# Up projections from seven products of halves instead of eight, the shared ones in the recurrent cell's PSUM banks, with program order kept to the end

## Chip, cores, metric

One core of a Trainium2 chip. The metric is the time of one execution in microseconds (us) on the device. A time "of n runs" is the median, with the lowest and highest behind it. All runs quoted were of the fast state except one run of `unpinned`, which is left out of its ratio. All times below are us unless another unit stands there; "step 20" is the pass of the main loop with s = 20 (counted from 0).

In the profile lines PE is TensorE (PEld its weight loads), DVE VectorE, ACT ScalarE, POOL GpSimd, SP the engine that issues most DMA; L92 is line 92 of the kernel. A record is one line of the trace: a 128x256 matmul leaves two. "Granted clock" is the share of full clock that TensorE was given.

## The reference

A gated recurrent cell (mLSTM) over 4 sequences of 768 tokens and 8 heads of 40 feeds a feed-forward block:

```python
def _moe_ref(x, w1, w2, w3, w_out):        # x: 3072 x 320, the output of the cell
    a = x @ w1                             # 320 x 1024
    b = x @ w2
    h = a * b @ w3                         # 1024 x 1024
    return (h @ w_out).astype(np.float32)  # 1024 x 320
```

The cell's part, cut to what matters: per token C = f C + i v k^T, then h = C q, a normaliser and an output gate. The kernel does it in chunks of 64 tokens with matmuls, and folds w3 @ w_out into one matrix of 1024 x 320 (`w3o`), so what is left of the feed-forward block is two "up" products, a product of the two, and one "down" product.

## The kernel before

TensorE's instructions are held in program order by the helper `mm`; the other engines' order is kept only up to the 17th step (`pinned`), after which a scheduler may move them. Two kinds of PSUM space matter: four banks in one tile `cell`, and four separate banks handed out in turn by `mps`.

```python
    cell = ps_c.tile([P, 4, 512], FP, name="cell", tag="cell")      # one tile, four banks
    ...
    def up(gr, fs, cs):                    # two blocks of 128 features, 256 tokens, both weights
        ...
        pa, pb = mps([128, len(fs), n], "pa"), mps([128, len(fs), n], "pb")
        for p, wt in ((pa, w1), (pb, w2)):
            for i, f in enumerate(fs):
                for cc in range(KF):       # 320 inputs = 128 + 128 + 64; the 64 come in up_rest
                    mm(p[:, i, :], wt[:, cc, f * 128:(f + 1) * 128], x[:, cc, cs], start=(i == cc == 0), stop=False)
        return pa, pb, x, gr, fs, cs

    def up_rest(pa, pb, x, gr, fs, cs):
        ...                                # the 64-row remainders, then
        nc.scalar.mul(out=a_sb, in_=pa, mul=UP ** -2)
        nc.vector.tensor_tensor(out=ab_t[gr][j][...], in0=pb, in1=a_sb, op=OP.mult)

    def ffn_out(gr, j):                    # a "down"
        po = mps([P, DM], "po")
        for f in range(FO):
            mm(po, ab_t[gr][j // 2][:, f, ...], w3o[:, f, :], start=(f == 0), stop=(f == FO - 1))
        o_sb = ffn.tile([P, DM], FP, name="o_sb", tag="o_sb", bufs=2)
        nc.scalar.copy(out=o_sb, in_=po)
        nc.scalar.dma_start(out=out[t0:t0 + P, :], in_=o_sb)
    ...
    n_up = [0] * 4 + [1] * 2 + [2] * 23 + [0]
    n_down = [0] * 17 + [2] * 10 + [0, 0, 4]
    pinned, ahead = 17, 9
    for s in range(len(n_up)):
        ...
        for _ in range(n_down[s]):
            ffn_out(*downs.pop(0))
        now = [ups.pop(0) for _ in range(n_up[s])]
        open_ups = [up(*x) for x in now]
        ...
        if s <= NU:
            gated = quarter_work(s, rest)  # the remainders, then the cell's matmuls and their readers
```

Of the kernel before, what the change touches and what calls it, by code (L numbers as in the profile page):

```python
# [8 lines left out]
FP = mybir.dt.float32  # L9
U32 = mybir.dt.uint32  # L10
AF = mybir.ActivationFunctionType
OP = mybir.AluOpType
UP = 2.0 ** 8
# [3 lines left out]
def kernel(  # L17
# [26 lines left out]
    nc = tc.nc  # L44

    B, H, S, D = q.shape
    L = 64
    P = 128
    NT = S // L
    NT2 = S // P  # L50
    NU = NT2 * B
# [3 lines left out]
    DM = H * D  # L55
    BH = B * H
    DFF = moe_w1.shape[1]
    FO = DFF // P
    KF = DM // P
    REM = DM - KF * P  # L60
    GT = B
    TG = GT * P
    NG = NU // GT
# [13 lines left out]
    def mps(shape, name):  # L77
        pool = banks.pop(0)
        banks.append(pool)
        return pool.tile(shape, FP, name=name, tag="m")  # L80
# [10 lines left out]
    def mm(out, lhsT, rhs, start=True, stop=True):  # L91
        in_order(nc.tensor.matmul(out, lhsT=lhsT, rhs=rhs, start=start, stop=stop))  # L92
# [4 lines left out]
    halves = [slice(0, L), slice(L, P)]  # L97
# [187 lines left out]
    def turn(n):  # L285


        if n >= N_DVE:
            for src, dst, name in zip(turned_in[n % 2], (kT_t, qT_t), ("kT", "qT")):
                dst[n] = sb.tile([128, NP, P], FP, name=name, tag=name)  # L290
                done = nc.vector.transpose(out=dst[n].rearrange("i p (r f) -> i p f r", f=4),
                                           in_=src[:, 32:TB].rearrange("i (p f d) -> i p f d", p=NP, f=4)[:, :, :, 0:32])
            return done
        for src, dst, name in ((kbuf[n % NB], kT_t, "kT"), (qbuf[n % NBQ], qT_t, "qT")):
            pt = mps([128, NP, P], "pt")
            for p in range(NP):
                transpose(pt[:, p, :], src[:, 2 * p:2 * p + 2, :].rearrange("p a b -> p (a b)"))
            dst[n] = sb.tile([128, NP, P], FP, name=name, tag=name)
            nc.scalar.copy(out=dst[n], in_=pt)
# [276 lines left out]
    def up_rest(pa, pb, x, gr, fs, cs):  # L576
        for i, f in enumerate(fs):
            for j, e in quarters:
                mm((pa, pb)[j][halves[e], i, :], wr[halves[j], f * 128 + e * L:f * 128 + (e + 1) * L],
                   x[halves[j], KF, cs], start=False, stop=(i == len(fs) - 1))  # L580
        j, t0 = divmod(cs.start, 2 * P)
        a_sb = ffn.tile([128, len(fs), cs.stop - cs.start], FP, name="a_sb", tag="a_sb")
        nc.scalar.mul(out=a_sb, in_=pa, mul=UP ** -2)  # L583
        nc.vector.tensor_tensor(out=ab_t[gr][j][:, fs[0]:fs[-1] + 1, t0:t0 + a_sb.shape[-1]], in0=pb, in1=a_sb, op=OP.mult)  # L584

    def ffn_out(gr, j):
        po = mps([P, DM], "po")
        for f in range(FO):
            mm(po, ab_t[gr][j // 2][:, f, j % 2 * P:(j % 2 + 1) * P], w3o[:, f, :], start=(f == 0), stop=(f == FO - 1))
        o_sb = ffn.tile([P, DM], FP, name="o_sb", tag="o_sb", bufs=2)  # L590
        nc.scalar.copy(out=o_sb, in_=po)  # L591
        t0 = j * S + gr * P
        nc.scalar.dma_start(out=out[t0:t0 + P, :], in_=o_sb)
# [1 line left out]

    ups = [(0, [f, f + 1], slice(j * 2 * P, (j + 1) * 2 * P)) for part in range(0, FO, FO // 2) for j in range(2)
           for f in range(part, part + FO // 2, 2)]
    ups += [(gr, [f, f + 1], slice(j * 2 * P, (j + 1) * 2 * P)) for gr in range(1, NG) for j in range(2)
            for f in range(0, FO, 2)]
    downs = [(gr, j) for gr in range(NG) for j in range(GT)]  # L600
    n_up = [0] * 4 + [1] * 2 + [2] * 23 + [0]
    n_down = [0] * 17 + [2] * 10 + [0, 0, 4]
    w12 = [("w12", i, part) for part in range(2) for i in range(2 * KF + 1)]
    todo = w12[KF * 2 + 1:] + [("wo", i, 0) for i in range(FO)] + [("w3", ko, part) for ko in range(FO) for part in range(2)]
    n_cvt = [2, 1, 1, 1, 2, 2, 3, 3, 3] + [2] * 7
    pinned, ahead = 17, 9
    behind = ExitStack()
    turned, converted, fetched = 0, 2, 2 * KF + 1

    for s in range(len(n_up)):  # L610
        if B <= s + 3 < NU:
            load_u(s + 3)
        if s + 2 < NU:
            load(s + 2)
            load_o(s + 2)
        if 0 < s < B - 1:
            weights(s + 1)
            out_gate(s)
        if s < NU:
            weighted(s)  # L620
            if s >= B:
                decayed(state[s % B][1], state[s % B][0], s, 0)
            if 0 < s < N_DVE:
                turn(s)
        if NY <= s - 2 < NU:
            send(s - 2)
        elif 0 <= s - 2 < NY:
            twice(s - 2)
        if NY <= s - 2 < NU:
            get_back(s - 2)  # L630
        while turned < min(s - 2, NY):
            x_trans(turned)
            turned += 1
        fold()
        for _ in range(n_down[s]):
            ffn_out(*downs.pop(0))
        now = [ups.pop(0) for _ in range(n_up[s])]
        open_ups = [up(*x) for x in now]
        if len(now) == 1 and turned == s - 2 < NY:
            x_trans(turned)  # L640
            turned += 1

        def rest():
            for x in open_ups:
                up_rest(*x)

        gated = None
        if s <= NU:
            gated = quarter_work(s, rest)
        else:  # L650
            rest()
        with tc.issue_after(gated.ins) if gated else nullcontext():
            if NY <= s - 2 < NU:
                x_turn(s - 2)
            if N_DVE <= s + 1 < NU:
                gated = turn(s + 1)
        if s == 0:
            gate_cols(g, gT, nc.scalar.copy)
            out_gate(0)
            scale_next()  # L660
            weights(1)
        if s == NU:
            cell_psum.close()
            banks.append(ctx.enter_context(tc.tile_pool(name="ps_x", bufs=4, space=bass.MemoryType.PSUM)))
        if B - 1 <= s < NU:
            if s + 1 < NU:
                weights(s + 1)
            out_gate(s)
        with tc.issue_after(gated.ins) if N_DVE <= s + 1 < NU else nullcontext():
            for _ in range(n_cvt[s] if s < len(n_cvt) else 0):  # L670
                convert()
                converted += 1
        if s >= ahead:
            while pend and len(scaled) < 2:
                scale_next()
        if N_DVE <= s + 2 < NU:
            load_turned(s + 2)
        while todo and fetched < converted + (2 if s < 2 else 3 if s < ahead - 1 else 4):
            fetch(*todo.pop(0))
            fetched += 1  # L680
        if s + 1 == pinned:
            for ins in keep_order(front):
                behind.enter_context(tc.issue_after(ins))
    behind.close()
    assert not ups and not downs and not todo and not pend and not turned_w3 and not ready_w3, (len(ups), len(downs), len(todo), len(pend))
# [1 line left out]
_INS = ['q', 'k', 'v', 'i_gate', 'f_gate', 'o_gate', 'moe_w1', 'moe_w2', 'moe_w3', 'moe_w_out']  # L687
_OUTS = [((3072, 320), 'float32')]
# [25 lines left out]
```

## Time and profile before

| | before |
|---|---|
| time, 3 runs (a fourth came with the result below) | 466.43 (465.67 to 467.24) |
| span of the profiled run | 464.6 |
| TensorE busy | 442.8 (95%) |
| VectorE busy | 262.6 (57%) |
| ScalarE busy | 134.4 (29%) |
| TensorE's share of the chain that ended last | 90% |

These lines are of the profile page of the kernel before: the slices (40 of 11.6 each, busy tenths), the granted TensorE clock in tenths, and the chain that ended last.

```profile
PE   2797989999999999999999999999999999999997
DVE  6758898899988988898823360624516134011110
PEclk9757999999999999999999999999999999999999
PE 90%; DVE 3%; SPq 2%; DMA 2%; issue 1%; POOL 1%; ACT 0%; ACTq 0%; DVEq 0%
```

From the seventh slice to the last but one TensorE has no gap that a tenth would show, and VectorE is lightly used in the second half. So TensorE's work is what the time consists of, and VectorE looks as if it had room. Both readings are right; neither says what happens when VectorE's results are asked for *between* two matmuls.

### The profile page before, as it was taken

Reading aid. Unit: us, or ns where it says so; the run is one execution under the profiler, and the core shown is the slowest. Engines: PE = TensorE matmul, PEld = TensorE weight load, DVE = VectorE, ACT = ScalarE, POOL = GpSimd, SP = SyncE. Lnnn points to the kernel's source line nnn. Section 1 sums busy time; section 2 is a strip of 40 time slices with the busy share of each in tenths; the row PEclk is TensorE's granted clock in tenths of the full one; section 3 lists DMA queues with packets and bytes.
Section 4 is the critical chain, followed back from the end, with each engine's and each line's share of the span. In section 5 each row is a group of like instructions: output and inputs, shape, how many; then the busy total and the mean of one; then the engine's idle time right before and its main releaser. Section 6 shows DMA issues by size and latency. Waiting matters only on the chain.

```text
span 464.6 us, 12788 instructions
## 1 busy us (share of the span) xinstructions
PE 442.8 (95%) x5319; PEld 356.1 (77%) x5319; DVE 262.6 (57%) x515; ACT 134.4 (29%) x376; POOL 82.6 (18%) x156
## 2 busy tenths in 40 slices
PE   2797989999999999999999999999999999999997
PEld 2686878888778887878778777787777877778864
DVE  6758898899988988898823360624516134011110
ACT  3743545444244134313641231211101101011110
POOL 5522333233220222022151120210000000000000
PEclk9757999999999999999999999999999999999999
DMA  8989978887988677676452635545021120200001
GB/s 174 182 163 173 204 156 159 158 194 174 204 185 195 151 141 171 171 153 141 89 134 58 142 65 123 111 92 118 17 64 32 32 64 1 62 16 14 1 14 44
DMA packets 136554, 52.72 MB, mean 113 GB/s; under 512 B 109936, under 2 KB 127536, under 8 KB 136496
## 3 DMA queue, kind: packets, MB, share of 16 engines
q1 hardware_dynamic: 132896, 47.87, 50.6%
q10 hardware_dynamic: 3600, 4.03, 2.5%
q8 instruction: 42, 0.69, 0.6%
q14 instruction: 16, 0.13, 0.1%
HBM read 46.07 MB, written 5.80 MB: 112 GB/s over the span
## 4 chain that ended last, share of the span: by engine, by line
PE 90%; DVE 3%; SPq 2%; DMA 2%; issue 1%; POOL 1%; ACT 0%; ACTq 0%; DVEq 0%
PE pa L92 27%; PE po L92 23%; PE pb L92 18%; PE cell L92 12%; PE wp L92 7%; DMA q_all<-in_q_dram 2%; PE pt L95 2%; SPq L128 1%; PE px L95 1%; SPq L173 1%; DVE h L380 0%; DVE pw L354 0%; POOL pw L282 0%; DVE h L376 0%; SPq L459 0%
## 5 line engine op out<-in xcount | busy, mean ns | idle before, releaser
L584 DVE TENSOR_TENSOR ab<-pb,a_sb 128x512 f32<-128x512 f32 x48 | 32.7, 689 | 137.7 <-ACT a_sb L583 137.6
L92 PE MATMUL po<-w3o,ab 128*128 128x320 f32 x384 | 106.2, 435 | 0.0
L92 PEld LDWEIGHTS po<-w3o,ab 128*128 128x128 f32 x384 | 72.1, 190 | 30.0 <-ACT a_sb L583 0.4
L92 PE MATMUL pa<-xT,w 128*128 128x256 f32 x384 | 91.0, 380 | 0.6 <-ACT xT L438 0.6
L92 PE MATMUL pb<-xT,w 128*128 128x256 f32 x384 | 90.7, 379 | 0.0
L92 PEld LDWEIGHTS pa<-xT,w 128*128 128x128 f32 x384 | 72.3, 190 | 13.0 <-ACT xT L438 0.9
L92 PEld LDWEIGHTS pb<-xT,w 128*128 128x128 f32 x384 | 73.0, 190 | 9.9
L583 ACT ACTIVATE a_sb<-pa 128x512 f32<-128x512 f32 x48 | 28.7, 598 | 172.0 <-PE pb L92 172.0
L309 POOL TENSOR_TENSOR state<-state,decay 128x164 f32<-128x164 f32 x40 | 19.3, 483 | 208.1 <-DVE den L388 157.8
L92 PE MATMUL pb<-xT,wr 64*64 64x256 f32 x384 | 47.0, 383 | 0.0
L92 PE MATMUL pa<-xT,wr 64*64 64x256 f32 x384 | 47.0, 383 | 0.0
L280 ACT ACTIVATE pw<-pw,aT 128x64 f32<-128x64 f32 x160 | 40.3, 336 | 15.8 <-DMA pw<-U_d 15.8
L92 PEld LDWEIGHTS pa<-xT,wr 64*64 64x64 f32 x384 | 25.8, 132 | 16.8 <-issue 7.8
L282 POOL TENSOR_SCALAR_AFFINE_SELECT pw<-pw 64x512 f32<-64x512 f32 x48 | 34.6, 722 | 14.3 <-ACT pw L280 12.7
L92 PE MATMUL wp<-wo,w3T 128*128 128x320 f32 x128 | 35.9, 433 | 1.1 <-DVE ab L584 1.1
L591 ACT COPY o_sb<-po 128x320 f32<-128x320 f32 x24 | 10.2, 423 | 78.8 <-PE po L92 74.9
L92 PEld LDWEIGHTS cell<-vbuf,pw 64*64 64x64 f32 x768 | 27.9, 143 | 6.1 <-DVE state L367 2.9
L92 PEld LDWEIGHTS wp<-wo,w3T 128*128 128x128 f32 x128 | 23.7, 190 | 10.2 <-DVE ab L584 1.4
L92 PE MATMUL cell<-vbuf,pw 64*64 64x41 f32 x768 | 27.9, 233 | 2.3 <-DVE state L367 2.3
L92 PEld LDWEIGHTS pb<-xT,wr 64*64 64x64 f32 x384 | 25.8, 132 | 0.0
L376 DVE TENSOR_TENSOR h<-cell,gT 128x328 f32<-128x328 f32 x24 | 12.0, 498 | 23.4 <-PE cell L92 23.4
L380 DVE TENSOR_TENSOR h<-cell,h 64x328 f32<-64x328 f32 x48 | 23.9, 497 | 1.1
(90 smaller groups left out, 465.7 us busy)
## 6 DMA issues: line engine op xcount, KB each, us to landing
raw<-in_moe_w_dram SPq DMA_DIRECT2D x64, 128.0 KB, 3.2
pw<-U_d SPq DMA_DIRECT2D x40, 128.0 KB, 3.9
kbuf<-in_k_dram SPq DMA_DIRECT2D x24, 160.0 KB, 4.5
vbuf<-in_v_dram SPq DMA_DIRECT2D x24, 160.0 KB, 4.8
o_in<-in_o_gate_dram SPq DMA_DIRECT2D x24, 160.0 KB, 4.5
out_dram<-o_sb ACTq DMA_DIRECT2D x24, 160.0 KB, 2.1
raw<-in_moe_w_dram SPq DMA_DIRECT2D x7, 512.0 KB, 5.8
raw<-in_moe_w_out_dram SPq DMA_DIRECT2D x32, 80.0 KB, 3.1
```

Source lines behind the costliest of these rows:

```text
L92: in_order(nc.tensor.matmul(out, lhsT=lhsT, rhs=rhs, start=start, stop=stop))
L95: in_order(nc.tensor.transpose(out, in_, ident[0:n, 0:n]))
L128: nc.sync.dma_start(out=dst, in_=rows(src, n))
L173: nc.sync.dma_start(out=dst, in_=src)
L280: nc.scalar.activation(out=pw[:, h, :], in_=src[:, h, :], func=AF.Exp, bias=aT[:, c, b * H + h:b * H + h + 1])
L282: nc.gpsimd.affine_select(out=pw[r], in_=pw[r], compare_op=OP.is_ge, fill=0.0, base=0, pattern=[[0, H], [1, L]], channel_multiplier=-1)
L309: nc.gpsimd.tensor_tensor(out=new, in0=old, op=OP.mult, in1=decay[:, b * NP:(b + 1) * NP, 2 * c + x:2 * c + x + 1] .to_broadcast([P, NP, D1]))
L376: nc.vector.tensor_tensor(out=h.rearrange("p (n two) d -> p two n d", two=2), in0=pi, in1=gT[:, c, hs].rearrange("p (n two) -> p two n", t ...
L380: nc.vector.tensor_tensor(out=h[r], in0=ph[x], in1=h[r], op=OP.add)
L583: nc.scalar.mul(out=a_sb, in_=pa, mul=UP ** -2)
L584: nc.vector.tensor_tensor(out=ab_t[gr][j][:, fs[0]:fs[-1] + 1, t0:t0 + a_sb.shape[-1]], in0=pb, in1=a_sb, op=OP.mult)
L591: nc.scalar.copy(out=o_sb, in_=po)
```

## The change

The intent: for the last three groups of 512 tokens, a 2 x 2 split of each up product (halves of the inputs, halves of the features against halves of the tokens) is done with seven products of halves instead of eight. Sums of weights and of tokens are formed ahead on VectorE. Three of the seven go straight into the result's banks ("single"); four are "shared" between several results: `p15` (a pair) and `p67` (a pair) per weight. They are read out, scaled and added by ScalarE and VectorE. The shared pairs need four more banks, and the change takes those of `cell`. What is read out is kept in the memory of the tile `wo`, and the sums lie in that of `raw` and `w3T`, so the profile shows these names. Program order is kept to the end (`pinned = 32`). The core of the diff, cut:

```diff
+        def shared():
+            p15, p67 = [bank(2 + j) for j in range(2)], [bank(j) for j in range(2)]
+            for j in range(2):
+                mm(p15[j][:, 0], of(j, 0, 0), B11, stop=False)
+                mm(p15[j][:, 1], sum_of(j, 0), T[0], start=False)
+                if j:
+                    nc.scalar.copy(out=kept[j][:, 0:4:3], in_=p15[j])                  # L646
+                else:
+                    nc.scalar.mul(out=kept[j][:, 0:4:3], in_=p15[j], mul=UP ** -2)     # L648
+            for j in range(2):
+                mm(p67[j][:, 0], sum_of(j, 1), T[1], stop=False)
+                mm(p67[j][:, 1], sum_of(j, 2), T[2], start=False)
+                for i in range(2):
+                    add(j, kept[j][:, 1 + i], p67[j][:, i], kept[j][:, i])             # L629, L631
+                nc.vector.tensor_tensor(out=kept[j][:, 1:4:2], ...)                    # L654
...
+        def product():
+            for t, a in zip(ab_t[gr], (lo, hi)):
+                nc.vector.tensor_tensor(out=t[...], in0=t[...], in1=a, op=OP.mult)     # L672
-    n_up = [0] * 4 + [1] * 2 + [2] * 23 + [0]
-    n_down = [0] * 17 + [2] * 10 + [0, 0, 4]
+    n_up = [0] * 4 + [1] * 2 + [2] * 11 + [0] * 15
+    n_seven = [0] * 19 + [1] * 12 + [0]
+    n_down = [0] * 17 + [2, 3, 2, 2, 2, 1] + [1] * 8 + [4]
-    pinned, ahead = 17, 9
+    pinned, ahead = 32, 9
...
+            if s <= NU:
+                seven[0]()          # single
+            seven[1]()              # shared
+        for i in range(n_down[s]):
+            ffn_out(*downs.pop(0), cell[:, 2 + i, 0:DM] if seven and s <= NU else None)
```

The line numbers in the comments were added here; the profile of the changed kernel names these lines. The last line matters: with the shared pairs in `cell`, the downs of these steps go into `cell` too.

More of the change, by code (lines that the diff above doesn't have):

```diff
@@ L584, in up_rest, with weight_sums @@
         nc.vector.tensor_tensor(out=ab_t[gr][j][:, fs[0]:fs[-1] + 1, t0:t0 + a_sb.shape[-1]], in0=pb, in1=a_sb, op=OP.mult)
-    def ffn_out(gr, j):
-        po = mps([P, DM], "po")
+    FH, TH = FO // 2, 2 * P
+    S_t, T_t = {}, {}
+    aside = wo.rearrange("p f d -> p (f d)")
+    def weight_sums(j):
+        mem = [wst.tile([128, CW, 2], U32, name="raw", tag="raw", bufs=4).rearrange("p n two -> p (n two)").bitcast(FP)
+               for _ in range(2)]
+        S1, S2, S3, S4 = S_t[j] = [m[:, i * CW:(i + 1) * CW] for m in mem for i in range(2)]
+        (A11, A21), (A12, A22) = ([(w1, w2)[j][:, cc, i * CW:(i + 1) * CW] for i in range(2)] for cc in range(KF))
+        for dst, p, q, op in ((S1, A21, A22, OP.add), (S2, S1, A11, OP.subtract), (S3, A11, A21, OP.subtract),
+                              (S4, A12, S2, OP.subtract)):
+            nc.vector.tensor_tensor(out=dst, in0=p, in1=q, op=op)
@@ new lines, in token_sums, with up_by_seven, of, sum_of @@
+    def token_sums(gr):
+        mem = wst.tile([128, FO, 128], FP, name="w3T", tag="w3T").rearrange("p k c -> p (k c)")
+        T1, T2, T3, T4 = T_t[gr] = [mem[:, i * TH:(i + 1) * TH] for i in range(4)]
+        (B11, B12), (B21, B22) = ([x_t[gr][:, cc, i * TH:(i + 1) * TH] for i in range(2)] for cc in range(KF))
+        for dst, p, q in ((T1, B12, B11), (T2, B22, T1), (T3, B22, B12), (T4, B21, T2)):
+            nc.vector.tensor_tensor(out=dst, in0=p, in1=q, op=OP.subtract)
+    def up_by_seven(gr, f, bank):
+        x, T = x_t[gr], T_t[gr]
+        (B11, B12), (B21, B22) = ([x[:, cc, i * TH:(i + 1) * TH] for i in range(2)] for cc in range(KF))
+        block, kept = {}, [aside[:, j * 4 * TH:(j + 1) * 4 * TH].rearrange("p (i t) -> p i t", i=4) for j in range(2)]
+        lo, hi = (ffn.tile([128, 2, TH], FP, name="a_sb", tag="a_sb") for _ in range(2))
+        def of(j, cc, i):
+            return (w1, w2)[j][:, cc, i * CW + f * 128:i * CW + (f + 1) * 128]
+        def sum_of(j, i):
+            return S_t[j][i][:, f * 128:(f + 1) * 128]
+        def add(j, out, p, q):
+            if j:
+                nc.vector.tensor_tensor(out=out, in0=p, in1=q, op=OP.add)
+            else:
+                nc.vector.scalar_tensor_tensor(out=out, in0=p, scalar=UP ** -2, in1=q, op0=OP.mult, op1=OP.add)
+        def single():
+            for j in range(2):
+                C1, C2 = block[j] = mps([128, 2, TH], "pa"), mps([128, 2, TH], "pb")
+                mm(C1[:, 0], of(j, 1, 0), B21, stop=False)
+                mm(C1[:, 1], of(j, 1, 1), T[3], start=False, stop=False)
+                mm(C2[:, 0], sum_of(j, 3), B22, stop=False)
+        def shared():
[3 more added lines that the diff above has]
+                mm(p15[j][:, 1], sum_of(j, 0), T[0], start=False)
+                if j:
+                    nc.scalar.copy(out=kept[j][:, 0:4:3], in_=p15[j])
+                else:
+                    nc.scalar.mul(out=kept[j][:, 0:4:3], in_=p15[j], mul=UP ** -2)
+            for j in range(2):
+                mm(p67[j][:, 0], sum_of(j, 1), T[1], stop=False)
+                mm(p67[j][:, 1], sum_of(j, 2), T[2], start=False)
+                for i in range(2):
+                    add(j, kept[j][:, 1 + i], p67[j][:, i], kept[j][:, i])
+                nc.vector.tensor_tensor(out=kept[j][:, 1:4:2], in0=kept[j][:, 1:3],
+                                        in1=kept[j][:, 3:4].to_broadcast([128, 2, TH]), op=OP.add)
+        def left():
+            if gr not in ab_t:
+                ab_t[gr] = [ffn.tile([128, FO, TH], FP, name="ab", tag="ab", bufs=6) for _ in range(2)]
+            for t in range(2):
+                for i in range(2):
+                    for j, e in quarters:
+                        c0 = (f + i * FH) * 128 + e * L
+                        mm(block[j][t][halves[e], i], wr[halves[j], c0:c0 + L], x[halves[j], KF, t * TH:(t + 1) * TH],
+                           start=False, stop=(i == 1))
+            for j, dst in enumerate(((lo, hi), [t[:, f:FO:FH, :] for t in ab_t[gr]])):
+                add(j, dst[0], block[j][0], kept[j][:, 0:3:2])
+                add(j, dst[1], block[j][1], kept[j][:, 1:4:2])
+        def product():
+            for t, a in zip(ab_t[gr], (lo, hi)):
+                nc.vector.tensor_tensor(out=t[:, f:FO:FH, :], in0=t[:, f:FO:FH, :], in1=a, op=OP.mult)
+        return single, shared, left, product
@@ L588, in ffn_out @@
+    def ffn_out(gr, j, po=None):
+        if po is None:
+            po = mps([P, DM], "po")
         for f in range(FO):
@@ L597 @@
            for f in range(part, part + FO // 2, 2)]
-    ups += [(gr, [f, f + 1], slice(j * 2 * P, (j + 1) * 2 * P)) for gr in range(1, NG) for j in range(2)
+    ups += [(gr, [f, f + 1], slice(j * 2 * P, (j + 1) * 2 * P)) for gr in range(1, 3) for j in range(2)
             for f in range(0, FO, 2)]
     downs = [(gr, j) for gr in range(NG) for j in range(GT)]
-    n_up = [0] * 4 + [1] * 2 + [2] * 23 + [0]
-    n_down = [0] * 17 + [2] * 10 + [0, 0, 4]
+    sevens = [(gr, f) for gr in range(3, NG) for f in range(FH)]
+    n_up = [0] * 4 + [1] * 2 + [2] * 11 + [0] * 15
+    n_seven = [0] * 19 + [1] * 12 + [0]
+    n_down = [0] * 17 + [2, 3, 2, 2, 2, 1] + [1] * 8 + [4]
     w12 = [("w12", i, part) for part in range(2) for i in range(2 * KF + 1)]
@@ L634 @@
         fold()
-        for _ in range(n_down[s]):
-            ffn_out(*downs.pop(0))
+        seven = None
+        if n_seven[s]:
+            seven = up_by_seven(*sevens.pop(0), (lambda i: cell[:, i].rearrange("p (i t) -> p i t", i=2)) if s <= NU else
+                                lambda i: mps([128, 2, TH], "p67" if i < 2 else "p15"))
+            if s <= NU:
[3 more added lines that the diff above has]
+            ffn_out(*downs.pop(0), cell[:, 2 + i, 0:DM] if seven and s <= NU else None)
+        if seven and s > NU:
+            seven[0]()
         now = [ups.pop(0) for _ in range(n_up[s])]
@@ L645, in rest @@
                 up_rest(*x)
+            if seven:
+                seven[2]()
         gated = None
@@ L652 @@
         with tc.issue_after(gated.ins) if gated else nullcontext():
+            if seven:
+                seven[3]()
             if NY <= s - 2 < NU:
@@ L656 @@
                 gated = turn(s + 1)
+            if s in (16, 17):
+                weight_sums(s - 16)
+            if s - 2 in range(4 * GT - 1, NU, GT):
+                token_sums((s - 2) // GT)
         if s == 0:
@@ L684 @@
     behind.close()
-    assert not ups and not downs and not todo and not pend and not turned_w3 and not ready_w3, (len(ups), len(downs), len(todo), len(pend))
+    assert not ups and not sevens and not downs and not todo and not pend and not turned_w3 and not ready_w3, (len(ups), len(downs), len(todo), len(pend))
 _INS = ['q', 'k', 'v', 'i_gate', 'f_gate', 'o_gate', 'moe_w1', 'moe_w2', 'moe_w3', 'moe_w_out']
```

## The prediction

> **What bounds the kernel now.** I read the page's engine summary first, then the chain that ended last in order of time, then the timeline of one step and of the tail. All times are us. TensorE is busy 95% of the span and carries 90% of the chain. From 230 on the chain is one unbroken row of TensorE work:
>
> ```profile
> 290.00 2.30 PE cell L92 x117
> 292.30 8.81 PE po L92 x32
> 301.11 1.73 PE pa L92 x8
> 302.83 1.73 PE pb L92 x8
> 304.56 1.73 PE pa L92 x8
> 306.29 1.73 PE pb L92 x8
> 309.90 2.29 PE cell L92 x104
> ```
>
> Columns: start, length, engine, tile, records. A step of this stage is 19.9: the recurrent cell 2.3, two down projections 8.81, two up blocks 6.9 and the 64-row remainders of the up blocks (309.90 less 308.02 = 1.88). Nothing waits, so each TensorE us saved there is a us of the end, and each new TensorE wait is one too. An up matmul of 128x256 is two records, eight records take 1.73: 0.432 per matmul. A down projection is 16 records, about 4.36 with its share of the gaps.
>
> The second thing to see is how the tile "cell" is waited for. It is one tile of four PSUM banks. Early in the run, where TensorE isn't backed up, the timeline shows:
>
> ```profile
> 37.67 1.01 DVE L380 TENSOR_TENSOR h<-cell,h 64x328 f32<-64x328 f32 x2
> ...
> 40.36 0.28 DVE L367 TENSOR_TENSOR state<-cell,state 128x164 f32<-128x164 f32 x1
> ...
> 40.69 1.83 PE L92 MATMUL cell<-vbuf,pw 64*64 64x41 f32 x30 [2.29 <-DVE state L367]
> ```
>
> The matmuls starting at 40.69 write banks 2 and 3, whose readers (L376, L380) had ended at 38.68. Yet they waited for L367, which reads bank 1. So the program orders accesses to cell as one tile, not bank by bank. In before this costs nothing later, because 17.6 of po, pa and pb stand between two uses of cell.
>
> Handoff costs, from the tail of the timeline:
>
> ```profile
> 443.98 17.49 PE L92 MATMUL po<-w3o,ab 128*128 128x320 f32 x64
> 444.10 0.60 ACT L583 ACTIVATE a_sb<-pa 128x512 f32<-128x512 f32 x1 [0.27 <-PE pb L92]
> ...
> 448.59 0.43 ACT L591 COPY o_sb<-po 128x320 f32<-128x320 f32 x1 [3.89 <-PE po L92]
> ```
>
> The first po takes to about 448.39 (443.98 + 0.1 + 4.31), its copy starts 448.59: 0.20 from TensorE to ScalarE. DVE to TensorE is 0.05 (40.64 to 40.69), and the first weight load after a wait costs about 0.1 more (a group at 425.99 took 1.83 for the usual 1.73). A 128x512 PSUM eviction on ScalarE is 0.60.
>
> [...] in 38 to 40 TensorE was busy 0.40 of 2.00 and in 42 to 44 the granted clock was 0.50, while an idle 1.5 around 61 left it at 1.00.
>
> **The change part by part.** *Removed:* each of the 12 new blocks (512 tokens, two weights) uses 14 products of 128x256 where two old steps' worth of the same work used 16; the remainders are equal. 24 x 0.432 = **10.4 off** TensorE. ScalarE loses 24 a_sb evictions.
>
> *Added on VectorE:* per block six shared adds (four of 256 columns, two of 512: 4 x 0.42 + 2 x 0.69 = 3.1), four adds of 512 (2.8), two products (1.4), less two old products (1.4): +5.9. With cell work 4.6 and turns 2.8 a step is about 14.6 on VectorE, beside 19.0 on TensorE with two downs (14 x 0.432 + 8.81 + 1.88 + 2.30), 14.6 with one. No throughput bound except near step 22, but order matters. Weight and token sums lie in steps 16, 17, 21, 25, beside TensorE work.
>
> *Moved:* there are now 32 steps. Six blocks (steps 19 to 24) put four pairs of shared products and the downs in cell's banks. I read the semaphore values in the built program: there each group waits for the reader of the group before, although in another bank. In order on TensorE:
> - first p15 waits for the last state add of the previous cell. In the step of 272 the cell's matmuls ended at 272.32, L359 at 274.98 and L367 at 275.98: 3.66 after (L367, steps 19 and 20) or 2.66 (L359, steps 21 to 24, where the second state isn't needed). TensorE arrives 2.59 after cell, with its six single products done: 1.2 or 0.2 with the 0.15 of a restart.
> - second p15 waits for ScalarE's copy of the first: 0.20 + 0.60 + 0.05 + 0.1 = 0.95.
> - first p67 waits for the copy of the second: 0.95.
> - second p67 waits for two adds of 256: 0.16 + 0.88 + 0.15 = 1.2.
> - first down waits for two more adds: 1.2.
> - second down waits for the first one's o_sb copy: 0.20 + 0.43 + 0.15 = 0.78.
>
> That is 4.3 per block, 5.1 with two downs, plus the state wait. VectorE may also be late for the first p67: it is needed about 8.5 after cell (7.5 from step 21) and is free after y 4.6, products 1.4, xT 0.57, kT and qT 2.2, so 8.7: 0.2 late at step 20, about 0.95 at steps 21 and 23; the token sums add 1.75 at step 22 (2.7 late). Steps 19 to 24: 6.3 + 6.5 + 6.2 + 7.2 + 5.4 + 4.5 = **36.1 of new TensorE waits**.
>
> After step 24 p15 and p67 are separate tiles, the waits are on readers a step old, and I find none that lasts, except: at step 25 the second p15 takes a bank of the closed cell and waits for the last h reads, 1.8; at the end the last downs need the last product (four adds of 0.69 and one product after the remainders), three matmuls of 0.54 cover part: 1.5. Keeping program order moves DMA issues, but the queue's work (about 12 a step) is less than a step, and every load is two steps ahead; I give it 0.
>
> Sum: 466.4 - 10.4 + 36.1 + 1.8 + 1.5 = 495.4.
>
> **The rivals.**
> 1. *The waits are hidden and the full gain shows:* 456. For it: VectorE and ScalarE are half idle in this stage (VectorE about 8 of 20). Against: the waits are round trips in TensorE's own order, with nothing independent placed between; idle engines don't shorten them.
> 2. *The clock falls.* Over the 7 to 8 us of shared products TensorE would be busy about 45%, and in the stretch around the second p67 nearer 30%. The trace has half clock after a stretch of such kind and none after one of about 55%. [...] I can't tell; I add an expected 3.
> 3. *VectorE becomes the bound.* At step 22, 14.6 plus 1.7 against 14.6 would make it so; that is in the sum as lateness. In steps 25 to 30 it has 7.3 beside 12.3.
> 4. *The waits are milder,* since ScalarE's or VectorE's turn-around is quicker or weights are loaded during a wait: 1 less per step would give 489.
>
> **Range and chances.** 495.4 + 3 gives 498. The low end (486) is a quarter of the waits missing, the high end (514) is a clock that falls in most of the six steps. Faster by 2% would need nearly the whole 10.4 and no wait; within 2% would need the 36 to be under 20.
>
> **What would show it.** Steps 19 to 24 should be 23 to 26 long with two downs and 18 to 22 with one; TensorE should be idle 0.8 to 1.2 ahead of cell matmuls, released by the ScalarE copies at L646/L648, the VectorE adds at L629/L631 and the o_sb copy. Its busy time should fall by about 10 and its idle time grow by about 40. Steps 25 to 30 should run 12.3 without waits. It is wrong if steps 19 to 24 run at 19.0 and 14.6 with no such waits, if the first p67 waits last several us (VectorE order), or if granted clock drops to 0.5 in this stage.

## The result, and the profile after

The changed kernel took 502.75 (499.01 to 504.96, 4 runs) against 466.05 (464.65 to 467.24, 4 runs) in the same rounds: ratio 1.078, 95% interval 1.071 to 1.085. Ratios here are the mean time of one kernel's fast runs over the mean of the other's fast runs of the same rounds, so they are not quite the ratio of the medians quoted. The change made the kernel slower, by 36.7 in the medians. The result was correct.

The same four rows of the page after:

```profile
PE   3879899999999999999996969796979799999997
DVE  7788698999889888898466372719285476555530
PEclk9975999999999999999999999899699999999999
PE 75%; DVE 15%; issue 3%; SPq 2%; ACT 1%; POOL 1%; DMA 1%; DVEq 0%; POOLq 0%; ACTq 0%
```

Three things are to be seen. TensorE now has six dips, in slices 22, 24, 26, 28, 30 and 32 (a slice is 12.4, so from 261 to 398): one for each step in which `cell` is shared. VectorE's share of the chain went from 3% to 15%, though it is busy only 68% of the span. And the clock row has two dents there (8 in slice 26, 6 in slice 29), where before had none.

The timeline of TensorE in step 19 of the changed kernel (start, length, tile, shape, records, and in brackets the idle time and what ended it) answers to the unbroken chain that the prediction shows:

```profile
261.86 0.70 PE L92 MATMUL cell<-xT,w 128*128 128x256 f32 x2 [0.85 <-DVE state L367]
262.39 0.59 PE L92 MATMUL cell<-w3T,raw 128*128 128x256 f32 x2
263.68 0.70 PE L92 MATMUL cell<-xT,w 128*128 128x256 f32 x2 [0.69 <-ACT wo L648]
264.21 0.59 PE L92 MATMUL cell<-w3T,raw 128*128 128x256 f32 x2
265.48 1.13 PE L92 MATMUL cell<-w3T,raw 128*128 128x256 f32 x4 [0.68 <-ACT wo L646]
267.66 1.13 PE L92 MATMUL cell<-w3T,raw 128*128 128x256 f32 x4 [1.05 <-DVE wo L631]
269.76 4.57 PE L92 MATMUL cell<-w3o,ab 128*128 128x320 f32 x16 [0.97 <-DVE wo L629]
274.85 4.57 PE L92 MATMUL cell<-w3o,ab 128*128 128x320 f32 x16 [0.52 <-ACT o_sb L682]
```

Every group waits for the reader of the group before it, though each stands in another bank (the first for the state add, the last reader of the cell): the second `p15` for ScalarE's copy of the first, the first `p67` for the copy of the second, the second `p67` and the first down for VectorE's adds, the second down for the copy of the first. The bracket shows only TensorE's idle time. What a wait costs the end is the start-to-start time less the work: the two `p15` start 1.82 apart (261.86, 263.68), and the first is two matmuls, 2 x 0.432 = 0.86 of work, so about 0.95 is lost, not 0.69. The rest is the end of the last matmul (a matmul of two records is 0.59 long, and in an unbroken row the next one starts 0.43 after it: 258.69 and 259.12) and the slower start of the first after a wait (0.70).

The waits of TensorE by releaser over the whole changed kernel (idle us in total, times, longest):

```profile
PE cell L92 <- DVE wo L631: 8.6, 6, 2.6
PE cell L92 <- DVE wo L629: 5.9, 6, 1.0
PE cell L92 <- ACT wo L648: 4.1, 6, 0.7
PE cell L92 <- ACT wo L646: 4.1, 6, 0.7
PE cell L92 <- ACT o_sb L682: 1.5, 3, 0.5
```

Each stands six times, once per shared step; the three copies of downs are the three steps with two downs. None of these rows exists before.

The clock. These are stretches of the changed kernel (stretch, length, then busy time of TensorE, its loads, VectorE, ScalarE, GpSimd, then the granted clock, DMA share and GB/s):

```profile
262.00:269.00 7.00, 4.38 (x16) 2.57 (x16) 5.22 (x9) 1.18 (x2) 2.06 (x3) 1.00 0.87 161
311.50:318.50 7.00, 4.51 (x18) 2.81 (x17) 6.79 (x15) 1.18 (x2) 0.00 (x0) 1.00 0.32 52
318.50:325.50 7.00, 6.02 (x13) 3.62 (x13) 1.98 (x4) 0.00 (x0) 0.00 (x0) 0.51 0.55 122
```

In the shared part of a step TensorE is busy about 4.4 of 7.0. In step 19 the clock stayed at 1.00. In step 21 it fell to a half just afterwards and stayed there for 7, under a down that then took 6.80 in place of 4.57. In this execution it fell twice (steps 21 and 22); the four records in question grew by 6.8 in all: second `p67` 1.72 and 2.07 where 1.13 is normal, first down 6.80 and 7.59 where 4.57 is.

From step 25 on, with `p15` and `p67` in separate tiles, TensorE waits once in step 25 (1.10, for L380) and once at the end (0.78, for L672), and not between. The chain there:

```profile
413.45 3.65 PE p L92 x16
...
425.89 3.65 PE p L92 x16
```

One step is 425.89 less 413.45 = 12.44, all TensorE.

### The profile page after: what moved, and what is told of

Read it like the earlier page. It is cut to its first block, busy times and chain, and to the rows that moved or that the text cites. A ratio compares the mean times of both kernels' runs of the same rounds, so it can differ in the third digit from the quotient of the medians.

```text
span 497.3 us, 12846 instructions
## 1 busy us (share of the span) xinstructions
PE 449.8 (90%) x5271; PEld 347.0 (70%) x5271; DVE 337.6 (68%) x655; ACT 135.2 (27%) x376; POOL 83.5 (17%) x156
## 3 DMA queue, kind: packets, MB, share of 16 engines
q1 hardware_dynamic: 132896, 47.87, 47.5%
## 4 chain that ended last, share of the span: by engine, by line
PE 75%; DVE 15%; issue 3%; SPq 2%; ACT 1%; POOL 1%; DMA 1%; DVEq 0%; POOLq 0%; ACTq 0%
PE cell L92 23%; PE pa L92 16%; PE po L92 13%; PE pb L92 10%; PE wp L92 7%; PE p L92 4%; DVE h L380 2%; DVE pw L354 1%; DVE ab L672 1%; PE pt L95 1%; DVE wo L629 1%; DVE h L376 1%; DVE wo L631 1%; SPq L137 1%; PE px L95 1%
## 5 line engine op out<-in xcount | busy, mean ns | idle before, releaser
L92 PE MATMUL po<-w3o,ab 128*128 128x320 f32 x240 | 66.5, 434 | 0.8 <-DVE ab L672 0.8
L92 PE MATMUL pa<-xT,w 128*128 128x256 f32 x240 | 62.2, 391 | 0.6 <-ACT xT L438 0.6
L631 DVE SCALAR_TENSOR_TENSOR a_sb<-pa,wo 128x512 f32<-128x512 f32 x12 | 8.3, 692 | 79.9 <-PE pa L92 79.9
L92 PEld LDWEIGHTS po<-w3o,ab 128*128 128x128 f32 x240 | 45.4, 190 | 19.6 <-DVE ab L672 1.3
L309 POOL TENSOR_TENSOR state<-state,decay 128x164 f32<-128x164 f32 x40 | 19.8, 494 | 201.1 <-DVE den L388 198.7
L92 PE MATMUL cell<-w3o,ab 128*128 128x320 f32 x144 | 46.4, 481 | 7.4 <-DVE wo L629 5.9
L92 PEld LDWEIGHTS pa<-xT,w 128*128 128x128 f32 x240 | 45.6, 195 | 8.7 <-ACT xT L438 1.1
L92 PEld LDWEIGHTS cell<-w3o,ab 128*128 128x128 f32 x144 | 29.6, 211 | 24.2 <-DVE wo L629 8.9
L92 PE MATMUL pb<-xT,w 128*128 128x256 f32 x192 | 45.5, 380 | 0.8 <-ACT kT L299 0.8
L92 PEld LDWEIGHTS pb<-xT,w 128*128 128x128 f32 x192 | 36.6, 191 | 6.2 <-ACT kT L299 1.2
L583 ACT ACTIVATE a_sb<-pa 128x512 f32<-128x512 f32 x24 | 14.4, 598 | 78.1 <-PE pb L92 78.1
L92 PE MATMUL cell<-w3T,raw 128*128 128x256 f32 x72 | 22.2, 421 | 12.7 <-DVE wo L631 8.6
L376 DVE TENSOR_TENSOR h<-cell,gT 128x328 f32<-128x328 f32 x24 | 11.9, 498 | 26.1 <-PE cell L92 26.1
```

The lines of the kernel that those rows point to most:

```text
L92: in_order(nc.tensor.matmul(out, lhsT=lhsT, rhs=rhs, start=start, stop=stop))
L309: nc.gpsimd.tensor_tensor(out=new, in0=old, op=OP.mult, in1=decay[:, b * NP:(b + 1) * NP, 2 * c + x:2 * c + x + 1] .to_broadcast([P, NP, D1]))
L376: nc.vector.tensor_tensor(out=h.rearrange("p (n two) d -> p two n d", two=2), in0=pi, in1=gT[:, c, hs].rearrange("p (n two) -> p two n", t ...
L631: nc.vector.scalar_tensor_tensor(out=out, in0=p, scalar=UP ** -2, in1=q, op0=OP.mult, op1=OP.add)
```

## The experiments

The kernel before was run beside each call on the same chip: 465.06 (463.57 to 468.68, 7 runs) for `split_cell`, `grouped`, `downs_first` and `both`, 465.32 (463.82 to 469.07, 15 runs) for `both_eight`, `unpinned`, `both_split` and `after_eight`, 465.95 (464.63 to 467.28, 11 runs) for the four with `_again`. The theory: each shared step loses its time in round trips TensorE to ScalarE or VectorE and back, because accesses to `cell` are ordered by whole tile and nothing else stands between; the clock adds to it. The rivals: only the tile's coarseness counts; VectorE is simply too busy; the kept program order does it; the removed products are worth less than counted.

### `split_cell`: cell as two tiles of two banks

```diff
-    cell = ps_c.tile([P, 4, 512], FP, name="cell", tag="cell")
+    cell = [ps_c.tile([P, 2, 512], FP, name=f"cell{i}", tag=f"cell{i}") for i in range(2)]
```

and the uses indexed accordingly: `p67` in the first tile, `p15` and the downs in the second.

> The cell as two tiles of two banks (0 and 1 for p67, 2 and 3 for p15 and the downs), all else as in the changed kernel. Theory (TensorE waits because the program orders accesses to cell by tile, not by bank): the first p67 no longer waits for the copy of p15 (0.95), the first down no longer for the p67 adds (1.2), and the first p15 only for the h reads; but the second p67 still waits for the adds of the first, and these stand behind the products and the kT and qT transposes on VectorE, so part of what is won is lost there: 1.2 to 2.4 us a step in steps 19 to 24, some 9 in all: about 492 to 494 beside 502. The first down should then wait for nothing and the copy L646 no longer release a p67. Rival (VectorE or ScalarE are simply short of time in these steps): no change, 500 to 504.

Measured: 483.75 (482.01 to 484.71), ratio 1.039 (1.034 to 1.044); correct. Of the five rows of waits above, two are gone (L629 and L646), that of the downs' copy is the same, and the others read:

```profile
PE cell L92 <- DVE wo L631: 11.8, 6, 3.2
PE cell L92 <- ACT wo L648: 4.1, 6, 0.7
```

So 19 of the 36.7 came, with the clock that it spared, from ordering two halves of the tile that share no bank. The saving went past what was expected. Two reasons can be read. The clock lost 3.4 in the 140 from 256 to 396, against 8.5 in the changed kernel (the sum over stretches of 1 us of one less the granted clock). And step 19 took 22.1 against 25.4, 3.3 less: besides the copy ahead of the first `p67` (0.95) and the adds ahead of the first down (1.24), the wait of the first `p15` for the state add (1.0) is gone too, as its tile is no longer the one that holds the state. What remains shows the next limit: the wait for L631 grew, up to 3.2, since the pair is now asked for while VectorE is still at the cell's outputs, the old block's products and the transposes.

### `grouped`: all shared products ahead of their readers, same tile

```diff
+            for j in range(2):
+                mm(p67[j][:, 0], sum_of(j, 1), T[1], stop=False)
+                mm(p67[j][:, 1], sum_of(j, 2), T[2], start=False)
             for j in range(2):
...
-                mm(p67[j][:, 0], sum_of(j, 1), T[1], stop=False)
-                mm(p67[j][:, 1], sum_of(j, 2), T[2], start=False)
```

(the new loop stands behind the four `p15` products, ahead of the copies).

> One tile of four banks as in the changed kernel, but all eight shared matmuls are issued before the first of their readers in program order, so that none of them waits for a reader of another bank. A plain sum of handoffs says that three of them go (0.95 + 0.95 + 1.2 in six steps, 18.6): 483. My theory says that the first down then waits for the last of all readers, and that this is the last of four VectorE adds (about 2.6 after VectorE comes free, at 8.4 to 8.7 after cell): 0.3 us less in most steps, 1 to 2 in steps 19 and 24, some 4 in all: about 498, with one wait of 3 to 5 us ahead of the first down in place of four short ones, and granted clock perhaps lower.

Measured: 502.11 (500.81 to 504.36), ratio 1.079 (1.073 to 1.086); correct. Its first shared step on TensorE:

```profile
263.49 2.32 PE L92 MATMUL cell<-w3T,raw 128*128 128x256 f32 x10
269.50 6.23 PE L92 MATMUL cell<-w3o,ab 128*128 128x320 f32 x16 [3.69 <-DVE wo L629]
```

Four waits became one, and the one is nearly as long as their sum: the down starts 6.01 after the first of five matmuls worth 2.16, so 3.85 is lost where the four waits of the changed kernel lost 4.45 in step 19. The first down must wait until VectorE has read both `p67`. The number of waits wasn't the cost; the reading that TensorE has to sit through was. The long gap also cost clock: it fell once in each of the six steps (6.23 for the down where 4.57 is normal), 13.6 in the same stretch, against 8.5. That eats what the shorter waits gave; the expectation had named it ("granted clock perhaps lower") but put no number to it.

### `downs_first`: the downs ahead, in their own banks

```diff
-    n_down = [0] * 17 + [2, 3, 2, 2, 2, 1] + [1] * 8 + [4]
+    n_down = [0] * 17 + [2, 3, 2, 1, 1, 2, 1] + [1] * 7 + [5]
...
-            if s <= NU:
-                seven[0]()
-            seven[1]()
         for i in range(n_down[s]):
-            ffn_out(*downs.pop(0), cell[:, 2 + i, 0:DM] if seven and s <= NU else None)
-        if seven and s > NU:
-            seven[0]()
+            ffn_out(*downs.pop(0))
+        if seven:
+            seven[1]()
+            seven[0]()
```

The downs follow the cell at once, in a bank of `mps`, then come the shared and last the single products. Their count per step changes because a down needs products of an earlier block; there are 24 as before. This changes two things at once, the place of the downs and their bank (`mps` in place of `cell`); which of the two frees the downs was not tested apart.

> The downs go ahead of the shared products, in banks of their own pool, and the single products behind them; one down is shifted to the end so that none waits for a fresh product. The readers stay between the shared matmuls. Theory: the waits ahead of the downs (1.2 and 0.78), on the state add, and VectorE's lateness go, the three handoffs inside the shared products stay (3.1 a step, six steps): 466 - 10.4 + 18.6 = 474. Rival (bank or engine contention): stays above 490.

Measured: 479.33 (475.66 to 482.17), ratio 1.029 (1.020 to 1.037); correct. The waits ahead of the downs are gone, those inside the shared group stay (L648 too, with 4.3):

```profile
PE cell L92 <- DVE wo L631: 6.3, 6, 1.1
PE cell L92 <- ACT wo L646: 4.1, 6, 0.7
```

All L631 waits are now the bare hand-off of about 1.05; VectorE's lateness is covered by the down. It is 5 above what was expected; the clock lost 5.1 in three falls, which the expectation had left out.

### `both`: downs ahead and shared products together

The two edits above in one kernel.

> The downs first and the shared matmuls ahead of all their readers; same arithmetic, same banks, same coarse tile. Theory: every wait by cell is now covered by at least 4.4 us of other TensorE work, so only the 24 matmuls saved are left: 466 - 10.4 = 456 (455 to 458), with TensorE without gaps from 230 on and granted clock 1.00. Rivals: the seven products cost something on TensorE that the waits hid (460 or more); VectorE's greater work is the bound (462 or more).

Measured: 457.18 (455.97 to 458.17), ratio 0.982 (0.977 to 0.987); correct. Here is the first shared step on TensorE, from the down to the next cell, and then the whole stretch:

```profile
258.75 8.88 PE L92 MATMUL po<-w3o,ab 128*128 128x320 f32 x32
...
268.76 2.32 PE L92 MATMUL cell<-w3T,raw 128*128 128x256 f32 x10
...
275.38 1.02 PE L92 MATMUL cell<-vbuf,pw 64*64 64x41 f32 x30
```

```profile
256.00:396.00 140.00, 140.00 (x1501) 109.92 (x1500) 104.54 (x204) 26.90 (x76) 15.21 (x22) 1.00 0.32 70
```

The same arithmetic, with the shared products still in the one tile `cell` (only the downs have left it), in another order, and every wait of the stage is gone: TensorE is busy 140.00 of 140.00 with the clock at 1.00. The read of the old cell passes under 8.7 of downs, the read of the shared products under the 2.7 of single products and 1.8 of remainders (270.92 to 275.38 in the timeline). VectorE is busy 104.5 of 140 there, so it was never the bound. This version beats both kernels, by 1.8% the kernel before; the whole interval is below 1, though not wholly below 0.98, so a gain of 2% is not established.

### `both_eight`: what the removed products are worth (wrong on purpose)

```diff
                 mm(C2[:, 0], sum_of(j, 3), B22, stop=False)
+                mm(C2[:, 0], sum_of(j, 3), B22, start=False, stop=False)
```

in `both`: one superfluous product per weight and block, 24 in all. The result is wrong, as intended.

> `both` (downs first, shared products together) with one superfluous product of 128x256 per weight and block, so 24 more matmuls, as many as the change removed; wrong on purpose. Our theory: with the waits gone TensorE alone sets the end, so each matmul costs its 0.432: 457.2 + 10.4 = 467.6 (466 to 469), a little above the kernel before. Rival: the sums on VectorE still set the end of some steps, so that part of the 24 hides beside them: 459 to 463.

Measured: 466.35 (465.03 to 468.14, 12 runs), ratio 1.002 (1.000 to 1.004). A step from 25 on took 13.30 in it (391.63 less 378.33 in its chain) against 12.44 in `both` (371.81 less 359.37): 0.86, two matmuls of 0.432. The profiled spans differ by 465.2 - 454.6 = 10.6, the medians by 9.2. So the 10.4 that the change took off TensorE was real, within the spread of the runs; and eight products in the new order give the time of the kernel before again, so the gain of `both` is that of the products removed.

### `unpinned`: order kept to the 17th step only

```diff
-    pinned, ahead = 32, 9
+    pinned, ahead = 17, 9
```

> The changed kernel with program order kept only as long as in the kernel before (up to the 17th piece), nothing else. Our theory: the order kept to the end isn't part of the loss; the waits sit between readers and matmuls that follow each other in the program anyway: 502.5, within 3 of the changed kernel. Rival: the kept order holds VectorE or ScalarE work back, and giving it up gains 5 or more.

Measured: 498.25 (493.46 to 502.15), ratio of the fast runs 1.066 (1.058 to 1.074); correct. The expectation (within 3 of the changed kernel) failed: the median of all four runs is 4.5 below the changed kernel as it was measured on another chip, that of the three fast ones (496.96) 5.8 below. The next two runs repeat the pair on one chip.

### `after_again` and `unpinned_again`: the pair on one chip

No edit; both kernels as above, in the same five rounds.

> The changed kernel unaltered, timed on the same chip and in the same rounds as the next run: 502.5, within 1.5 of its first measurement.

> As `unpinned`, beside the changed kernel. If the 4.5 seen across chips was spread of the clock's falls, this is within 2 of after_again (500 to 503). Rival: keeping the order does cost, about 4 (498), where VectorE's work ahead of the first shared pair is held back.

Measured: 501.69 (497.87 to 503.51, 6 runs), ratio 1.075 (1.072 to 1.079), and 497.20 (495.12 to 502.55, 6 runs), ratio 1.069 (1.065 to 1.073). The medians are 4.5 apart again, the means 3.2, and the two intervals overlap; with the two pairs together (10 runs against 9 fast ones) the means are 4.1 apart. So the rival held: the kept order does cost something. Two parts can be shown. The first is the end of the changed kernel, on VectorE and TensorE:

```profile
476.88 0.68 DVE L629 TENSOR_TENSOR ab<-pb,wo 128x512 f32<-128x512 f32 x1
477.48 1.28 DVE L672 TENSOR_TENSOR ab<-ab,a_sb 128x512 f32<-128x512 f32 x2
...
478.22 15.88 PE L92 MATMUL po<-w3o,ab 128*128 128x320 f32 x58 [0.78 <-DVE ab L672]
```

and of `unpinned`:

```profile
474.42 0.68 DVE L629 TENSOR_TENSOR ab<-pa,wo 128x512 f32<-128x512 f32 x1
475.13 0.69 DVE L672 TENSOR_TENSOR ab<-ab,a_sb 128x512 f32<-128x512 f32 x1
...
474.55 17.50 PE L92 MATMUL po<-w3o,ab 128*128 128x320 f32 x64
```

In program order all four adds come first, then both products. The scheduler of `unpinned` takes the adds of the first half of the tokens, its product, then the other half; the first product is ready after two adds, and the last downs run through as 64 records without a wait. From the product of step 25 that waited to the end of the last down the changed kernel took 92.27 (401.84 to 494.11) and `unpinned` 91.23: 1.04. The second part lies in the shared steps. In step 20 of `unpinned` (first line VectorE, second TensorE):

```profile
290.04 1.29 DVE L672 TENSOR_TENSOR ab<-ab,a_sb 128x512 f32<-128x512 f32 x2
295.05 1.13 PE L92 MATMUL cell<-w3T,raw 128*128 128x256 f32 x4 [1.05 <-DVE wo L631]
```

The wait for L631 is 1.05 where the changed kernel has 1.68; in step 22 it is 2.31 for 2.58, and that for L380 at step 25 is 0.84 for 1.10: 1.16 in all. The second profiles of the two kernels give 1.11 in the same way, from the first single product of step 19 to step 25 less the longer records. So 2.2 of the difference is waits, in both pairs of profiles, of which the first differ by 2.0 (497.3 and 495.3) and the second by 4.4 (500.6 and 496.2). The rest goes with the clock: in the 140 from 256 to 396 the loss was 8.5 and 11.1 in the two profiles of the changed kernel, and 6.8 in both of `unpinned`, where each of four falls lasted about 3.4; in the changed kernel they lasted 6.8 and 10.2 in one profile, 3.4 once and 6.8 three times in the other. Why another order on the other engines should make the falls shorter these runs don't settle.

### `both_split`, `both_again`, `both_split_again`: the coarse tile where nothing waits

The edit of `split_cell` on top of `both`, then both kernels on one chip.

> `both` with cell as two tiles of two banks. Our theory: a tile too coarse costs only where nothing else stands between reader and next matmul; in `both` TensorE was 100% busy in the stage, so nothing is gained: 457.2, within 1.5. Rival: the coarse tile still costs hidden time in other steps: 455 or less.

> As `both`, unaltered, on the same chip and in the same rounds as the next run: 457.2, within 1.

> As `both_split`, beside both_again. If the coarse tile costs nothing with other work between, within 0.7 of it; rival: 1.5 to 2 less, as the two runs on different chips had it.

Measured: 455.63 (455.52 to 456.06), ratio 0.978 (0.974 to 0.983); then 456.87 (455.75 to 458.25), ratio 0.981 (0.979 to 0.983), beside 455.54 (454.54 to 456.79), ratio 0.978 (0.976 to 0.980); all correct. The split gives 1.3 in the medians of the pair (the intervals overlap) and 1.6 across chips, where within 0.7 and within 1.5 had been expected: a little past both expectations, and short of both rivals. It isn't in the shared stage: from the cell ahead of the first shared step to the start of the last downs the chain takes 173.12 in both (256.36 to 429.48, and 255.85 to 428.97). Of the 0.7 by which these two profiles differ 0.5 was there before 256, where `both` waits 2.0 for the state add (L367) and `both_split` doesn't. In the second pair of profiles the split kernel comes to this stage 0.6 later instead (259.40 and 258.78 at the first down), so where the 1.3 lies stays open.

### `after_eight`: two more products in the changed kernel (wrong on purpose)

The edit of `both_eight` in the changed kernel.

> The changed kernel with one superfluous product of 128x256 per weight and block put back among the single products, wrong on purpose. Our theory: in steps 20 to 23 the first p67 waits for VectorE, so extra TensorE work ahead of it is partly free there; about two thirds of the 10.4 show: 507 to 510, or 1 to 3 less where busier TensorE keeps its clock up. Rival: TensorE work adds in full everywhere: 513.

Measured: 507.73 (504.94 to 509.01), ratio 1.091 (1.084 to 1.097); the wrong result was intended. 10.4 of TensorE work cost only 5.0, in medians from two chips. The waits explain it: with 0.86 more work ahead of it the first `p15` of step 19 no longer waits for the state add, the longest wait for L631 is 1.9 in place of 2.6, and the clock lost 5.1 in place of 8.5. Part of TensorE's work in these steps lies beside waits, so adding to it doesn't show in full; that removing it wouldn't either was not tested.

## Why the prediction was right, point by point

The class (slower) and the size (498 predicted, 502.75 measured, inside 486 to 514) held. By its steps:

**Ten off TensorE.** Right, and shown by `both_eight`: 10.6 in the profiles, 0.86 per step. (The list of parts has ScalarE losing 24 evictions and leaves out the 24 copies of `p15` that it gains: it was busy 134.4 before and 135.2 after.)

**The round trips.** Right, nearly to the digit. Start-to-start losses in step 19: first `p15` 1.0 (predicted 1.2), second `p15` 0.95 (predicted 0.95), first `p67` 1.80 - 0.86 = 0.94 (0.95), second `p67` 2.18 - 0.86 = 1.32, of which 1.2 was predicted, first down 2.10 - 0.86 = 1.24 (1.2), second down 5.09 - 4.31 = 0.78 (0.78). Whole steps, from the end of one cell's matmuls to the end of the next: 25.4, 26.1, 27.3, 24.8, 19.4, 18.4 in steps 19 to 24, where 25.3, 25.5, 25.2, 21.8, 20.0 and 19.1 follow from the prediction's terms. Steps 21 and 22 are those in which the clock fell, by 2.8 and 4.0 of longer records; without that they would be 24.5 and 20.9; with it they lie above the ranges that were given as a sign (23 to 26, and 18 to 22), as step 20 does by 0.1.

**VectorE's lateness.** Mis-sized. For steps 21 to 23 it was put at 0.95, 2.7 and 0.95; the second `p67` of step 22 waited 2.58 where a bare hand-off waits 1.05, so it was 1.5 late, and those of steps 21 and 23 waited 1.13 and 1.12, so they were hardly late at all. Single records were sized well: 0.42 was put down for an add of 256 columns, which `before` has for its 96x256 records (L522, L539), and L629 and L631 took 0.42 for 128x256 in the changed kernel; the 0.69 of 512 columns is L584 of `before` (689 ns). The prediction added up whole records of VectorE, but most start before the record ahead of them ends: in step 22 the pair of products, the three transposes and the four token sums take 1.21, 2.31 and 1.45 from start to start (341.14, 342.35, 344.66, 346.11), where 1.4, 2.77 and 1.75 were summed; that is 0.95 of the 1.2 too much. At step 20 it was put at 0.2 and was 0.6 (1.68 less 1.05). That one has a visible cause. On VectorE and GpSimd in step 20:

```profile
288.53 2.09 DVE L672 TENSOR_TENSOR ab<-ab,a_sb 128x512 f32<-128x512 f32 x2
```

```profile
288.35 0.85 POOL L304 TENSOR_TENSOR vw<-vbuf,wT 128x328 f32<-128x328 f32 x1
289.16 0.91 POOL L309 TENSOR_TENSOR state<-state,decay 128x164 f32<-128x164 f32 x1
```

and in step 21, with GpSimd idle at that time:

```profile
313.81 1.28 DVE L672 TENSOR_TENSOR ab<-ab,a_sb 128x512 f32<-128x512 f32 x2
```

The pair of products takes 0.8 longer beside GpSimd's two operations, and GpSimd's own L309 takes 0.91 where it took 0.46 in step 19 (263.71). In `unpinned`, where GpSimd does these at other times, the pair of step 20 takes 1.29 and the lateness is gone.

**The clock.** It fell as rival 2 had it (from 256 to 396 the loss was 8.5 in the changed kernel, 13.6 in `grouped`, 6.8 in `unpinned`, 5.1 in `downs_first` and in `after_eight`, 3.4 in `split_cell`, and there was none in `before`, `both`, `both_eight` and `both_split`, where TensorE has no such waits), but the term was too small: 3 was put down, and the records in the profiled run grew by 6.8. The two stretches of `before` that rival 2 compares with read: TensorE busy 0.40 of 2.00 from 38 to 40 and the clock at 0.50 from 40.4 on; busy 2.33 of 4.00 (58%) from 60 to 64 and the clock at 1.00. What the falls would cost in the new stage was not shown by them: the 3, and the 514 of the high end, were the author's estimate. In the second profile of the changed kernel the clock fell in four of the six steps and the same count gives 10.2. Take these off and the two executions stand at 499.01 - 6.8 = 492.2 and 502.39 - 10.2 = 492.2: the kernel without its clock is the same in both, and the spread of the changed kernel (497.87 to 504.96 over ten runs) is, in these two, the clock's. The prediction's sum without a clock, 495.4, was 3 too high, and its clock term about 4 to 7 too low; they partly cancelled, and that the total came within 5 owes something to this luck. The 3 can be found: the six steps' hand-offs come to 29.0, the state adds to 2.3 and the lateness to 2.3, together 33.7 of the 36.1 put down, and step 25 and the tail (below) are 1.0 short. By the prediction's last list a clock of 0.5 in this stage was a sign of being wrong; it came, so that sign went against the prediction although its path held. What sets off a fall stays open: ahead of the one in step 21 no gap of TensorE was over 1.13, with TensorE busy 4.51 of 7.00 (311.5 to 318.5); in step 19, with the same waits, the clock stayed at 1.00 in the first profile and fell in the second (`after_again`: 0.50 from 268.0 to 274.5, after 3.59 busy of 6.00).

**Step 25 and the tail.** The late start at step 25 is there (released by L380): 401.84 less 400.14 less 0.43 gives 1.27, where 1.8 was put down. The tail cost 1.04 where 1.5 was put down.

**"Keeping program order ... I give it 0."** This step failed, in a small way: it looked at the DMA queue alone. Order kept on the other engines costs 4.5 in the medians of one chip (3.2 in the means); 1.04 of it is the tail, which the prediction charged to the last product itself, about 1.1 is longer waits in steps 20, 22 and 25, and the rest follows the clock.

**Rivals 1, 3 and 4.** Hidden waits (456): the changed kernel doesn't hide them, but `both` shows at 457 that the estimate for hidden waits was right and that the order of TensorE's program, with the downs in banks of their own, decides it. VectorE as the bound of the stage: refuted, since `both` has 104.5 of VectorE work in 140 and TensorE doesn't wait. Milder waits: by 0.4 a step (33.7 against 36.1), not by 1.

**What would show it.** The releasers came as named. One sign was wrong: TensorE's busy time was to fall by 10 and its idle time to grow by 40. It rose from 442.8 to 449.8, and the idle time grew from 21.8 to 47.5. A wait makes the matmuls around it look longer (the last record's end no longer overlaps the next, 0.16, and the first starts slower, 0.11); for the 29 or so waits that is about 8, and the clock's 6.8 counts as busy too. Together that is most of the 17 between 432.4 and 449.8.

## What to carry to other kernels

Before a buffer is borrowed, look at what stands between its last reader and its next writer on the bound engine: here four free banks lay in one tile whose accesses are ordered as a whole, and a borrower that writes, waits and writes again lost 0.78 to 1.32 per group in step 19; two tiles in place of one brought 502.75 to 483.75. The saving on the bound engine came out only when its program was arranged so that independent work lies across each round trip: the same arithmetic gave 503 in one order and 457 in another. And count idle time of TensorE twice: with TensorE busy about 4.4 of 7.0 in a shared stretch the clock fell in some of the steps, which cost 6.8 in one profile and 10.2 in another.
